# A fixed instruction order on every engine, a shorter distance between attention and input product, and an earlier set-up

## The chip, the cores and the metric

The kernel runs on one core of one Trainium2 chip. The metric is the device time of one execution in microseconds (us). A timed comparison has four runs of the kernel and four to seven runs of the kernel before, on the same chip. A ratio is the mean time of one kernel's fast runs over that of the other's of the same rounds, so it is not quite the ratio of the medians that are quoted beside it. The experiments ran on four chips, on which the kernel before took 435.4 to 436.0 us (medians); a difference between experiments of less than about 1 us is not read.

The names of the engines: PE is TensorE (PEld its weight loads), DVE is VectorE, ACT is ScalarE, POOL is GpSimd, SP is SyncE, which only issues transfers here.

## The reference, cut to what matters

```python
# r, k, v: (4, 8, 768, 48), w, u: (8, 48)
for t in range(S):
    cur = einsum('bhd,bhe->bhde', u * k_t, v_t)
    y_t = einsum('bhd,bhde->bhe', r_t, state + cur)
    state = w * state + einsum('bhd,bhe->bhde', k_t, v_t)
# y as (3072, 384); then
h = x @ w_in                       # 384 -> 1024
solu = h * softmax(h)
ln = (solu - mean) / sqrt(var + 1e-6) * g_ln
out = ln @ w_out                   # 1024 -> 384
```

The attention is done in 24 chunks of 128 tokens (four sequences of six). The two weight matrices arrive in 64-bit floating point and are converted on the chip, in 14 pieces.

## The kernel before

One round of the main loop handles attention chunk i, the input product and softmax of chunk i-LA, and the transposes and output product of chunk i-LA-LO. The parts that matter (cuts marked with "..."):

```python
LA, LO = 5, 3
psH = ...   # one buffer: the input product h_ps, 128x1024, fills it
psM = ...   # four buffers, shared by all other products and transposes but the scores

def convert(j):                                  # one weight piece
    nc.scalar.activation(out=mag, in_=hi..., func=ACT.Abs)            # ACT
    nc.vector.tensor_scalar(out=mag, ...)                             # DVE, clamp
    nc.vector.tensor_scalar(out=ma, ...)                              # DVE, shift
    nc.vector.scalar_tensor_tensor(out=ma, ...)                       # DVE, sign
    nc.scalar.activation(out=low, in_=lo, ...)                        # ACT
    if f is None:                                                     # w_in
        nc.gpsimd.tensor_tensor(out=dst..., in0=ma, in1=low, op=ALU.add)
    else:                                                             # w_out
        nc.gpsimd.tensor_tensor(out=ma, in0=ma, in1=low, op=ALU.add)  # POOL
        nc.scalar.activation(out=dst, in_=ma..., scale=g_sb[...])     # ACT, scaling

def weigh(i):
    nc.gpsimd.tensor_mul(kp..., kt..., kdec...)          # decayed k
    nc.gpsimd.tensor_mul(rku, kt[:, :, 0:D], u_bc)       # r*k*u, two products
    nc.gpsimd.tensor_mul(rku, rku, rt[:, :, 0:D])
    nc.vector.tensor_reduce(out=own[:, :, 0], in_=rku, ...)           # and their sum
    for h in range(H):                                   # eight diagonals: each token's own score, by head
        nc.scalar.activation(out=AT[:, h, :], in_=ident, scale=own[:, h])
...
with tc.manual_schedule(engines={mybir.EngineType.PE}):
    for i in range(-2, N + LA + LO):
        j, l = i - LA, i - LA - LO
        ...   # load(i+4), weigh(i+3), turn(i+2), conversions, then
        ...   # turn_ln(l), ffn_in(j), scores(i+1), ffn_out(l), finish(i)
```

`manual_schedule(engines={PE})` means: TensorE executes in the order of the program text, and a scheduler orders the instructions of the other engines.

## Time and profile before

| | before |
|---|---|
| time, median of 3 | 436.07 us |
| span of the profiled run | 433.0 us |
| mean granted TensorE clock | 0.991 |
| TensorE dense from | 102.07 us |
| one full round of TensorE | 16.08 us |

From the profile page of the kernel before, the busy times with their share of the span, and the chain of work that ended last, by engine:

```profile
PE 386.2 (89%) x2853; PEld 244.0 (56%) x2853; DVE 214.7 (50%) x386; ACT 181.6 (42%) x422; POOL 133.2 (31%) x165
...
PE 77%; POOL 8%; DVE 6%; issue 3%; ACT 2%; SPq 2%; DMA 1%; POOLq 0%; ACTq 0%; DVEq 0%
```

TensorE is the main bound: the chain runs through it for 77% of the span. What can be won without shortening TensorE's own work lies in the first quarter, where TensorE has holes; the other engines' shares are low on average but not there. The prediction below shows the slices and the table by stretch that say so.

### The profile page before, as it was taken

To read this page: it belongs to the slowest core of one execution; us is meant where nothing else is said; L and a number is where in the kernel's file an instruction comes from. 1 tells how busy PE (TensorE), PEld (TensorE's weight loads), DVE (VectorE), ACT (ScalarE), POOL (GpSimd) and SP (SyncE) were. 2 spreads that over 40 slices of the span, in tenths; PEclk is the share of its full clock that TensorE was granted. 3 is DMA by queue.
4 is the path that set the end of the run, shared out by engine and by line. 5 is a ranking of instruction groups with operands and counts; after the bars stand their busy time and mean duration, and the time that the engine had idled before them with its cause. 6 is when DMAs were issued, how large, how long until landed. Compare 5 with 4: busy or idle time off the path is not lost.

```text
span 433.0 us, 7179 instructions
## 1 busy us (share of the span) xinstructions
PE 386.2 (89%) x2853; PEld 244.0 (56%) x2853; DVE 214.7 (50%) x386; ACT 181.6 (42%) x422; POOL 133.2 (31%) x165
## 2 busy tenths in 40 slices
PE   0178692878999999999999999999999999999994
PEld 0167462445656656656756756756655565555662
DVE  5749885987453552552552542642544244444310
ACT  1667656765335435434434434533422233333310
POOL 5377686686134134134124113201000000000000
PEclk9999998899999999999999999999999999999999
DMA  9997989223033033033033011000000000000011
GB/s 147 232 242 148 157 193 173 27 56 56 20 56 74 18 56 73 20 56 73 20 55 73 24 34 38 20 2 18 20 0 20 20 20 18 18 18 19 0 39 42
DMA packets 81592, 25.92 MB, mean 60 GB/s; under 512 B 76557, under 2 KB 79758, under 8 KB 81550
## 3 DMA queue, kind: packets, MB, share of 16 engines
q1 hardware_dynamic: 80364, 25.17, 29.7%
q8 instruction: 24, 0.39, 0.4%
q10 hardware_dynamic: 1186, 0.20, 0.4%
q14 instruction: 18, 0.15, 0.1%
HBM read 20.65 MB, written 4.72 MB: 59 GB/s over the span
## 4 chain that ended last, share of the span: by engine, by line
PE 77%; POOL 8%; DVE 6%; issue 3%; ACT 2%; SPq 2%; DMA 1%; POOLq 0%; ACTq 0%; DVEq 0%
PE o_ps L737 29%; PE h_ps L698 27%; PE y_ps L668 7%; PE t_ps L726 5%; PE at L640 4%; PE kv_ps L684 3%; POOL kp L607 3%; POOL rku L612 2%; PE tr_ps L625 1%; POOL rku L611 1%; PE tk_ps L629 1%; DMA rpad<-in_r_dram 1%; DVE AT L643 1%; ACT AT L617 1%; SPq L462 1%
## 5 line engine op out<-in xcount | busy, mean ns | idle before, releaser
L698 PE MATMUL h_ps<-w_in_sb,xT 128*128 128x512 f32 x288 | 129.3, 599 | 11.7 <-DVE solu L708 11.7
L737 PE MATMUL o_ps<-w_out_sb,lnT 128*128 128x384 f32 x384 | 129.2, 490 | 0.0
L737 PEld LDWEIGHTS o_ps<-w_out_sb,lnT 128*128 128x128 f32 x384 | 71.5, 190 | 49.0 <-issue 2.4
L698 PEld LDWEIGHTS h_ps<-w_in_sb,xT 128*128 128x128 f32 x288 | 53.5, 193 | 70.4 <-issue 70.4
L704 ACT ACTIVATE e<-h_ps,st 128x1024 f32<-128x1024 f32 x24 | 26.7, 1114 | 116.9 <-DVE st L702 116.9
L713 POOL TENSOR_SCALAR st<-st 128x1 f32<-128x1 f32 x24 | 4.6, 192 | 193.3 <-ACT sq L712 193.1
L617 ACT ACTIVATE AT<-ident,own 128x128 f32<-128x128 f32 x192 | 59.1, 391 | 8.3 <-DVE own L614 8.3
L702 DVE TENSOR_REDUCE st<-h_ps 128x1 f32<-128x1024 f32 x24 | 29.4, 1223 | 60.3 <-PE h_ps L698 60.3
L712 ACT ACTIVATE sq<-solu,st 128x1024 f32<-128x1024 f32 x24 | 27.6, 1149 | 44.0 <-DVE st L710 44.0
L716 DVE TENSOR_SCALAR solu<-solu,st 128x1024 f32<-128x1024 f32 x24 | 21.5, 896 | 43.9 <-POOL st L715 43.9
L607 POOL TENSOR_TENSOR kp<-kpad,kdec 128x512 f32<-128x512 f32 x24 | 31.1, 1301 | 36.1 <-PE kv_ps L684 32.3
L640 PEld LDWEIGHTS at<-rT,kT 48*128 48x128 f32 x384 | 24.7, 189 | 22.9 <-issue 15.5
L640 PE MATMUL at<-rT,kT 48*128 48x128 f32 x384 | 30.0, 287 | 7.0 <-DVE AT L643 6.7
L614 DVE TENSOR_REDUCE own<-rku 128x8 f32<-128x384 f32 x24 | 13.1, 548 | 39.8 <-POOL rku L612 39.8
L643 DVE COPY_PREDICATED AT<-later,at 128x512 f32<-128x512 uint32 x48 | 32.3, 723 | 0.5 <-PE at L640 0.5
L708 DVE SCALAR_TENSOR_TENSOR solu<-h_ps,st,e 128x1024 f32<-128x1024 f32 x24 | 30.8, 1283 | 0.8
L612 POOL TENSOR_TENSOR rku<-rku,rpad 128x384 f32<-128x384 f32 x24 | 25.1, 1050 | 18.2 <-DMA rpad<-in_r_dram 17.5
L611 POOL TENSOR_TENSOR rku<-kpad,u_bc 128x384 f32<-128x384 f32 x24 | 25.9, 1079 | 7.0 <-DMA kpad<-in_k_dram 7.0
L726 PE MATMUL t_ps<-ident,solu 128*128 128x128 f32 x192 | 25.3, 274 | 1.7 <-DVE st L710 1.2
L668 PE MATMUL y_ps<-AT,vt 128*32 128x128 f32 x768 | 25.5, 273 | 0.0
L726 PEld LDWEIGHTS t_ps<-ident,solu 128*128 128x128 f32 x192 | 21.7, 141 | 5.2 <-issue 2.2
L684 PE MATMUL kv_ps<-vt,kp 128*128 128x96 f32 x160 | 22.6, 284 | 0.8 <-DVE state L690 0.8
(65 smaller groups left out, 358.7 us busy)
## 6 DMA issues: line engine op xcount, KB each, us to landing
kpad<-in_k_dram SPq DMA_DIRECT2D x24, 192.0 KB, 4.1
rpad<-in_r_dram SPq DMA_DIRECT2D x24, 192.0 KB, 5.0
vt<-in_v_dram SPq DMA_DIRECT2D x24, 192.0 KB, 3.0
out_dram<-o SPq DMA_DIRECT2D x24, 192.0 KB, 1.9
raw<-in_moe_w_in_dram SPq DMA_DIRECT2D x6, 512.0 KB, 5.2
raw<-in_moe_w_out_dram SPq DMA_DIRECT2D x8, 384.0 KB, 3.6
u_bc<-in_u_dram ACTq DMA_DIRECT2D x1, 192.0 KB, 3.8
g_sb<-in_moe_g_ln_dram ACTq DMA_DIRECT2D x1, 4.0 KB, 5.7
```

The lines of the kernel that those rows point to most:

```text
L607: nc.gpsimd.tensor_mul(kp.rearrange("p h d -> p (h d)"), kt.rearrange("p h d -> p (h d)"), kdec.rearrange("p a d -> p (a d)"))
L611: nc.gpsimd.tensor_mul(rku, kt[:, :, 0:D], u_bc)
L612: nc.gpsimd.tensor_mul(rku, rku, rt[:, :, 0:D])
L617: nc.scalar.activation(out=AT[:, h, :], in_=ident, func=ACT.Copy, scale=own[:, h])
L640: nc.tensor.matmul(pss[q][:, a, :], X["kT"][rows, a, :], X["rT"][rows, a, :], start=True, stop=True)
L643: nc.vector.copy_predicated(A4[:, :, q, :], later.to_broadcast([128, HP, T]), pss[q])
L668: nc.tensor.matmul(y_ps[32 * g : 32 * g + 32, j, :], lhsT, rhs, start=(g not in opened), stop=stop, skip_group_check=True)
L684: nc.tensor.matmul(kv_ps[:, a], pair(X["kp"], a), vt[:, 2 * a : 2 * a + 2, 0:D], start=True, stop=True)
L698: nc.tensor.matmul(h_ps[:, ts(n, NX)], X["xT"][:, j, :], w_in_sb[:, j, ts(n, NX)], start=(j == 0), stop=(j == KD - 1))
L708: nc.vector.scalar_tensor_tensor(out=solu, in0=h_ps, scalar=rs, in1=e, op0=ALU.mult, op1=ALU.mult, accum_out=tot)
L726: nc.tensor.transpose(t_ps[:, f, :], X["solu"][:, ts(4 * g + f, 128)], ident)
L737: nc.tensor.matmul(o_ps, X["lnT"][:, f, :], w_out_sb[:, f, :], start=(f == 0), stop=(f == KF - 1))
```

## The change

Its intent: take the order of all engines out of the scheduler's hands, so that the tables are made while GpSimd rests and the w_in pieces are converted first; and bring the input product from five chunks behind attention to two, so that full rounds begin three rounds sooner. (The decay row was the first transfer in the text before, too; the scheduler issued it third, at 2.19 us.) Its core:

```diff
-    LA, LO = 5, 3
+    LA, LO = 2, 3
+    ctx.enter_context(tc.manual_schedule())
...
+    nc.sync.dma_start(out=wq[:, :, 0:D], in_=w...)      # decay row: now the first transfer
...
-    load(0, "kr"); ...; load_weights(0); load(1, "v"); load(2); load_weights(1); ...
+    load(0, "kr"); load_weights(0); load(1, "kr"); load(0, "v"); load_weights(1); ...
...
+    double(0)                     # decay table for k first, then its transposes,
+    ...                           # then reciprocals and double(1), the table for r
...
-    with tc.manual_schedule(engines={mybir.EngineType.PE}):
-        for i in range(-2, N + LA + LO):
+    conversions = {-2: 1, -1: 1, 0: 2, 1: 2, 2: 3, 3: 3, 4: 2}
+    for i in range(-2, N + LA + LO):
+        ...                                  # load, turn_r
+        if i <= 0: weigh_own(i + 2, nc.vector)
+        turn_k(i + 2)
+        decay_k(i + 3)
+        for _ in range(conversions.get(i, 0)): convert(todo.pop(0)); ...
+        diagonal(i + 2)
+        turn_ln(l)
+        ffn_in(j)                            # input product, maximum, exponential
+        scores(i + 1)
+        unit(j)                              # reciprocal, product, square, root
+        weigh_own(i + 3, nc.gpsimd)          # two products, and DVE's sum
+        ffn_out(l)
+        normalise(j)
+        finish(i)                            # attention product, copy xT, state
```

In the changed kernel this text is the queue of every engine.

More of the change, by code (lines that the diff above doesn't have):

```diff
@@ L451, in direct_path @@
     vts = [const.tile([128, H, D + 32], F32, name=f"vt{i}") for i in range(NV)]
-    for i in range(NLD):
-        nc.vector.memset(kpads[i][:, :, D:P], 0.0)
-        nc.vector.memset(rpads[i][:, :, D:P], 0.0)
-    for vt in vts:
-        nc.gpsimd.memset(vt[:, :, D:], 0.0)
     def load(i, which="krv"):
@@ L472, in direct_path @@
     nc.vector.memset(wq, 1.0)
+    nc.sync.dma_start(out=wq[:, :, 0:D], in_=w.rearrange("(a q) d -> a q d", q=2))
+    nc.scalar.dma_start(out=u_bc.rearrange("p h d -> p (h d)"),
+                        in_=u.rearrange("h d -> (h d)").partition_broadcast(128))
+    for i in range(NLD):
+        nc.vector.memset(kpads[i][:, :, D:P], 0.0)
+        nc.vector.memset(rpads[i][:, :, D:P], 0.0)
     def words(x):
@@ L517, in convert @@
                                  scale=g_sb[:, f : f + 1])
-    nc.sync.dma_start(out=wq[:, :, 0:D], in_=w.rearrange("(a q) d -> a q d", q=2))
     load(0, "kr")
-    nc.scalar.dma_start(out=u_bc.rearrange("p h d -> p (h d)"),
-                        in_=u.rearrange("h d -> (h d)").partition_broadcast(128))
+    load_weights(0)
     load(1, "kr")
     load(0, "v")
-    load_weights(0)
+    load_weights(1)
     load(1, "v")
-    load(2)
-    load_weights(1)
+    load_weights(2)
+    load(2, "kr")
+    load_weights(3)
+    load(2, "v")
+    load_weights(4)
     load(3)
-    load_weights(2)
-    nc.scalar.dma_start(out=g_sb, in_=moe_g_ln.rearrange("(c p) -> p c", p=128))
-    nc.scalar.dma_start(out=wrow, in_=w.rearrange("h d -> (h d)").partition_broadcast(1))
     ident = const.tile([128, 128], F32, name="ident")
     make_identity(nc, ident)
+    for vt in vts:
+        nc.gpsimd.memset(vt[:, :, D:], 0.0)
     neg_half = const.tile([128, 1], F32, name="neg_half")
-    nc.vector.memset(neg_half, -0.5)
+    nc.gpsimd.memset(neg_half, -0.5)
     tab = const.tile([128, 2, HP, T], F32, name="tab")
@@ L544, in direct_path, with double @@
     pw = const.tile([128, 2, 8, HP], F32, name="pw")
+    nc.vector.memset(back[:, :, T - 1 : T], 1.0)
+    def double(x):
+        for j in range(7):
+            n = 1 << j
+            nc.vector.tensor_mul(tab[:, x, :, T - 2 * n : T - n], tab[:, x, :, T - n : T],
+                                 pw[:, x, j].unsqueeze(2).to_broadcast([128, HP, n]))
     wd_ps = psM.tile([128, HP], F32, tag="m", name="wd_ps")
     nc.tensor.transpose(wd_ps, wq.rearrange("a q d -> a (q d)"), ident[0:HP, 0:HP])
-    nc.vector.memset(back[:, :, T - 1 : T], 1.0)
     nc.vector.tensor_scalar(out=pw[:, 0, 0], in0=wd_ps, scalar1=LOW, scalar2=HIGH,
@@ L551, in direct_path @@
         nc.vector.tensor_mul(pw[:, 0, j + 1], pw[:, 0, j], pw[:, 0, j])
-    nc.vector.reciprocal(out=pw[:, 1], in_=pw[:, 0])
-    nc.vector.tensor_copy(out=fore[:, :, T - 1 : T], in_=pw[:, 1, 0].unsqueeze(2))
-    for j in range(7):
-        n = 1 << j
-        step = pw[:, :, j].unsqueeze(3).to_broadcast([128, 2, HP, n])
-        nc.vector.tensor_mul(tab[:, :, :, T - 2 * n : T - n], tab[:, :, :, T - n : T], step)
+    double(0)
     kdec = const.tile([128, HP, 128], F32, name="kdec")
@@ L564, in direct_path @@
     nc.scalar.copy(out=kdec, in_=kd_ps)
+    nc.vector.reciprocal(out=pw[:, 1], in_=pw[:, 0])
+    nc.vector.tensor_copy(out=fore[:, :, T - 1 : T], in_=pw[:, 1, 0].unsqueeze(2))
+    double(1)
     later = const.tile([128, 1, T], U32, name="later")
@@ L571, in direct_path, with make_wt @@
                             pattern=[[1, T]], channel_multiplier=-1)
-    nc.vector.tensor_copy(out=later[:, 0, :], in_=mf)
+    nc.gpsimd.tensor_copy(out=later[:, 0, :], in_=mf)
+    states = [const.tile([128, HP, 2, D], F32, name=f"state{b}") for b in range(B)]
     wt = const.tile([128, HP, 2, D], F32, name="wt")
-    nc.gpsimd.memset(wt, 0.0)
-    for q in range(2):
-        rows = slice(q * P, q * P + D)
-        nc.vector.tensor_copy(out=wt[rows, :, q, :],
-                              in_=pw[rows, 0, 7].unsqueeze(2).to_broadcast([D, HP, D]))
-    states = [const.tile([128, HP, 2, D], F32, name=f"state{b}") for b in range(B)]
+    def make_wt():
+        nc.gpsimd.memset(wt, 0.0)
+        for q in range(2):
+            rows = slice(q * P, q * P + D)
+            nc.gpsimd.tensor_copy(out=wt[rows, :, q, :],
+                                  in_=pw[rows, 0, 7].unsqueeze(2).to_broadcast([D, HP, D]))
     bad = flag.tile([1, 1], mybir.dt.int32, name="bad")
     def check_range():
+        nc.sync.dma_start(out=wrow, in_=w.rearrange("h d -> (h d)").partition_broadcast(1))
         ok = small.tile([1, dm], F32, tag="ok", name="ok", bufs=1)
@@ L600, in pair, with decay_k, weigh_own, diagonal @@
         return t[:, 2 * a : 2 * a + 2, :].rearrange("p q d -> p (q d)")
-    def weigh(i):
-        kt, rt = kpads[i % NLD], rpads[i % NLD]
+    def decay_k(i):
         X = live[i] = {}
-        X["kp"] = kp = apool.tile([128, H, P], F32, name="kp", bufs=4)
-        nc.gpsimd.tensor_mul(kp.rearrange("p h d -> p (h d)"),
-                             kt.rearrange("p h d -> p (h d)"),
+        X["kp"] = apool.tile([128, H, P], F32, name="kp", bufs=4)
+        nc.gpsimd.tensor_mul(X["kp"].rearrange("p h d -> p (h d)"),
+                             kpads[i % NLD].rearrange("p h d -> p (h d)"),
                              kdec.rearrange("p a d -> p (a d)"))
+    def weigh_own(i, engine):
         rku = apool.tile([128, H, D], F32, name="rku")
-        nc.gpsimd.tensor_mul(rku, kt[:, :, 0:D], u_bc)
-        nc.gpsimd.tensor_mul(rku, rku, rt[:, :, 0:D])
-        own = small.tile([128, H, 1], F32, name="own")
+        engine.tensor_mul(rku, kpads[i % NLD][:, :, 0:D], u_bc)
+        engine.tensor_mul(rku, rku, rpads[i % NLD][:, :, 0:D])
+        own = live[i]["own"] = small.tile([128, H, 1], F32, name="own")
         nc.vector.tensor_reduce(out=own[:, :, 0], in_=rku, axis=AX.X, op=ALU.add)
-        AT = X["AT"] = apool.tile([128, H, T], F32, name="AT", bufs=4)
+    def diagonal(i):
+        X = live[i]
+        AT = X["AT"] = apool.tile([128, H, T], F32, name="AT", bufs=3)
         for h in range(H):
-            nc.scalar.activation(out=AT[:, h, :], in_=ident, func=ACT.Copy, scale=own[:, h])
-    def turn(i):
-        X, rt = live[i], rpads[i % NLD]
-        X["kT"] = apool.tile([128, HP, T], F32, name="kT")
-        X["rT"] = apool.tile([128, HP, T], F32, name="rT", bufs=3)
+            nc.scalar.activation(out=AT[:, h, :], in_=ident, func=ACT.Copy, scale=X["own"][:, h])
+    def turn_r(i):
+        rT = live[i]["rT"] = apool.tile([128, HP, T], F32, name="rT", bufs=3)
         ps = psM.tile([128, HP, T], F32, tag="m", name="tr_ps")
         for a in range(HP):
-            nc.tensor.transpose(ps[:, a, :], pair(rt, a), ident)
-        nc.vector.tensor_mul(X["rT"], ps, fore)
+            nc.tensor.transpose(ps[:, a, :], pair(rpads[i % NLD], a), ident)
+        nc.vector.tensor_mul(rT, ps, fore)
+    def turn_k(i):
+        X = live[i]
+        X["kT"] = apool.tile([128, HP, T], F32, name="kT")
         ps = psM.tile([128, HP, T], F32, tag="m", name="tk_ps")
@@ L700, in ffn_in @@
         st = small.tile([128, 8], F32, name="st")
-        nmax, se, rs, tot, nmu, ss, var, rstd = (st[:, n : n + 1] for n in range(8))
+        nmax, se, rs, tot, nmu, ss, var, rstd = X["st"] = [st[:, n : n + 1] for n in range(8)]
         nc.vector.tensor_reduce(out=nmax, in_=h_ps, axis=AX.X, op=ALU.max, negate=True)
@@ L704, in ffn_in, with unit @@
         nc.scalar.activation(out=e, in_=h_ps, func=ACT.Exp, bias=nmax, accum_out=se)
+        X["h"], X["e"] = h_ps, e
+    def unit(i):
+        X = live[i]
+        nmax, se, rs, tot, nmu, ss, var, rstd = X["st"]
+        h_ps, e = X["h"], X["e"]
         nc.vector.tensor_scalar_add(rs, se, 1e-9)
@@ L715, in ffn_in, with normalise @@
         nc.gpsimd.tensor_tensor(out=rstd, in0=var, in1=neg_half, op=ALU.pow)
-        nc.vector.tensor_scalar(out=solu, in0=solu, scalar1=nmu, scalar2=rstd,
+    def normalise(i):
+        X = live[i]
+        nmax, se, rs, tot, nmu, ss, var, rstd = X["st"]
+        nc.vector.tensor_scalar(out=X["solu"], in0=X["solu"], scalar1=nmu, scalar2=rstd,
                                 op0=ALU.add, op1=ALU.mult)
@@ L745, in direct_path @@
     todo = list(range(len(pieces)))
-    count = {5: 3, 6: 3, 7: 2}
-    ahead = 3
-    weigh(0)
-    weigh(1)
-    with tc.manual_schedule(engines={mybir.EngineType.PE}):
-        for i in range(-2, N + LA + LO):
-            j, l = i - LA, i - LA - LO
-            if 0 <= i and i + 4 < N:
-                load(i + 4)
-            if 0 <= i + 3 and i + 3 < N and i + 3 >= 2:
-                weigh(i + 3)
-            if 0 <= i + 2 < N:
-                turn(i + 2)
-            for _ in range(count.get(i, 1)):
-                if i >= -1 and todo:
-                    convert(todo.pop(0))
-                if ahead < len(pieces):
-                    load_weights(ahead)
-                    ahead += 1
-            if i == 10:
-                check_range()
-            if 0 <= l < N and i < N + LA:
-                turn_ln(l)
-            if 0 <= j < N:
-                ffn_in(j)
-            if 0 <= i + 1 < N:
-                scores(i + 1)
-            if N + LA - 1 <= i < N + LA + LO - 1:
-                turn_ln(l + 1)
-            if 0 <= l < N:
-                ffn_out(l)
-            if 0 <= i < N:
-                finish(i)
+    ahead = 5
@@ new lines, in direct_path @@
+    conversions = {-2: 1, -1: 1, 0: 2, 1: 2, 2: 3, 3: 3, 4: 2}
+    decay_k(0)
+    for i in range(-2, N + LA + LO):
+        j, l = i - LA, i - LA - LO
+        drain = i >= N + LA - 1
+        if 0 <= i and i + 4 < N:
+            load(i + 4)
+        if i + 2 < N:
+            turn_r(i + 2)
+            if i <= 0:
+                weigh_own(i + 2, nc.vector)
+            turn_k(i + 2)
+        if i + 3 < N:
+            decay_k(i + 3)
+        if i == -2:
+            make_wt()
+        for _ in range(conversions.get(i, 0)):
+            convert(todo.pop(0))
+            if ahead < len(pieces):
+                load_weights(ahead)
+                ahead += 1
+        if i + 2 < N:
+            diagonal(i + 2)
+        if i == 0:
+            nc.sync.dma_start(out=g_sb, in_=moe_g_ln.rearrange("(c p) -> p c", p=128))
+        if i == 10:
+            check_range()
+        if 0 <= l and not (drain and i > N + LA - 1):
+            turn_ln(l)
+        if 0 <= j < N:
+            ffn_in(j)
+        if 0 <= i + 1 < N:
+            scores(i + 1)
+        if 0 <= j < N:
+            unit(j)
+        if 0 <= i and i + 3 < N:
+            weigh_own(i + 3, nc.gpsimd)
+        if drain and l + 1 < N:
+            turn_ln(l + 1)
+        if 0 <= l:
+            ffn_out(l)
+        if 0 <= j < N:
+            normalise(j)
+        if 0 <= i < N:
+            finish(i)
```

## The prediction

> **What bounds the kernel now.** I read the page from the top: busy shares, slices, then the chain of waits, then who waited for whom, then each engine's instructions in order of time for the first 105 us and for one round of the middle.
>
> ```profile
> PE   0178692878999999999999999999999999999994
> DVE  5749885987453552552552542642544244444310
> PEclk9999998899999999999999999999999999999999
> DMA  9997989223033033033033011000000000000011
> ```
>
> One slice is 10.8 us. From the tenth on, TensorE is full; the ten before it are the ramp, where TensorE has holes and DVE, ACT, GpSimd and the DMA are busy in turn. The busy table by stretch puts numbers to it (columns: PE, PE weight loads, DVE, ACT, POOL busy, clock, DMA share, GB/s).
>
> ```profile
> 0.00:19.07 19.07, 0.24 (x2) 0.18 (x2) 14.12 (x42) 7.02 (x19) 9.34 (x21) 1.00 1.12 180
> 19.07:56.50 37.43, 28.45 (x374) 24.06 (x375) 26.12 (x41) 25.21 (x65) 26.50 (x22) 1.00 0.99 193
> 56.50:102.07 45.57, 33.35 (x316) 21.37 (x315) 35.79 (x62) 28.78 (x71) 34.09 (x34) 0.93 0.52 93
> 102.07:310.70 208.63, 207.47 (x1597) 130.93 (x1597) 97.75 (x170) 87.82 (x209) 57.30 (x72) 1.00 0.21 41
> 310.70:427.40 116.70, 116.67 (x572) 67.46 (x568) 40.91 (x72) 32.28 (x58) 5.93 (x16) 1.00 0.06 19
> ```
>
> So after 102.07 us nothing but TensorE's own work counts, and before it everything else does. One full round of TensorE, from the chain of waits: transposes of the output side 0.87, input product 5.15, scores 1.09, output product 5.36, attention product 1.67, state product 1.06, transposes of r and k 0.44 each, together 16.08 us. In the ramp TensorE waited for:
>
> ```profile
> PE h_ps L698 <- DVE solu L708: 11.7, 2, 8.8
> PE kd_ps L563 <- DVE tab L557: 11.5, 1, 11.5
> PE wd_ps L546 <- POOL rku L611: 7.3, 1, 7.3
> PE at L640 <- DVE AT L643: 6.7, 4, 2.6
> ```
>
> The first 19 us are table making; the last hole is the input product waiting for the softmax of the chunk before it, which holds its only PSUM tile.
>
> **What the skill says.** "PSUM — Partial Sum Buffer", section "Engine vs sequencer instructions": the queues of ScalarE, VectorE and GpSimd are strictly first in, first out. The trace of before can't contradict it, since a scheduler chose the order there; under a fixed order it means that one instruction which waits stops all written after it. "SBUF — State Buffer", section "SBUF: two separate sides": VectorE and GpSimd share a port pair as an exclusive lock. The trace agrees: the clamp of a weight piece takes 0.43 us alone and 1.50 us when it starts at 33.34 beside a GpSimd product that ends at 34.55. "TensorE: Matmul & The Clock Gate", section "What's actually happening": after an idle window TensorE runs at half clock for about 3.4 us. Here the input product after the 8.8 us hole took 6.96 us, the next ones 5.3.
>
> **The change part by part.** Round i holds attention chunk i; the input product is now of chunk i-2 (before i-5), the output product still three behind it. So full rounds begin at round 5, not 8. TensorE's work from the start of round 5 on: 15 full rounds (5 to 19) 241.1, then rounds that lose the state product, transposes, scores and attention, 15.0+15.0+14.1+13.0+11.2+12.1+6.0+6.0+5.2 = 97.6, together 338.7. (Check by the same sum for before: 12 full rounds and 131.2 make 324.1; 102.07 plus 1.3 of waits plus 324.1 is 427.5, measured 427.4.) After it come 5.6 us of eviction and store, and the time is 3.1 above the profiled span (436.07 against 433.0). The time after is T5 + 338.7 + waits + 8.7, and the change gains only if round 5 starts before 88.7 us less any new waits.
>
> *Start.* The decay row is now the first transfer on its queue (before: 2.19 us, behind 384 KB, used at 7.26), so I take it at 4.2. GpSimd only clears buffers then, so the seven squarings cost 0.19 each, not 0.56, and seven half-size doublings about 2.0: the first table at 8.2 in place of 19.07, its transposed copy at 10, the first scores at 13 (before 24.96). About 11 us gained.
>
> *Rounds 0 and 1.* DVE runs in program order: turned r 0.68, for the first three chunks also two products (0.55 each) and the sum (0.55), conversions of a w_in piece 1.53 each, masks 1.34, the sum of r·k·u, which from chunk 3 on waits for GpSimd (two weight additions 1.27 each, then two products 1.05 each), the state 0.54. With the port lock I get the end of DVE's round 0 at 33, of round 1 at 43. TensorE's first input product ends near 40.5 (before 63.4).
>
> *Rounds 2 to 4: the w_out conversions.*
>
> ```profile
> L501 ACT ACTIVATE mag<-raw 128x384 f32<-128x384 f32 x8 | 4.4, 546 | 0.0
> L502 DVE TENSOR_SCALAR mag<-mag 128x384 f32<-128x384 f32 x8 | 5.7, 714 | 2.7 <-ACT mag L501 2.6
> L508 DVE SCALAR_TENSOR_TENSOR ma<-raw,ma 128x384 uint32<-128x384 uint32 x8 | 7.0, 870 | 0.1
> L515 POOL TENSOR_TENSOR ma<-ma,low 128x384 uint32<-128x384 uint32 x8 | 8.1, 1017 | 6.5 <-DVE ma L508 3.3 <-ACT low L511 2.0 <-DVE st L706 1.0
> L516 ACT ACTIVATE w_out_sb<-ma,g_sb 128x384 f32<-128x384 f32 x8 | 4.9, 612 | 5.3 <-POOL ma L515 5.3
> ```
>
> Each piece goes ACT, DVE, GpSimd, ACT. In the fixed order ACT does magnitude, low word, scaling of one piece before the magnitude of the next, and the scaling waits for GpSimd. So pieces no longer overlap: 0.55 + 0.36 + 0.35 + 0.56 (uncontended) + 1.0 + 0.61 and some 0.25 of hops is 3.7 us each. Behind them in the same queues stand, in order, DVE's maximum 1.22; ACT's eight diagonals 2.45 after the last scaling; the exponential 1.3; DVE's reciprocal and product 1.75; ACT's square 1.35; GpSimd's variance and root 0.85, two products 2.1; DVE's sum, normalisation and state 2.0. A round with three pieces: 0.7 + 1.3 to the first addition + 1.05 + 0.65 + 2 x 3.7 + 2.45 + 1.3 + 1.75 + 1.35 + 0.85 + 2.1 + 2.0 = 22.9; with two, 19.2. DVE's rounds 2, 3, 4 end at about 66, 89, 108. TensorE needs 10 us in each and waits for the product that frees the input product's PSUM tile: the input products start near 59, 82 and 101 to 104, the last being the one of round 5. Taking 1.75 of transposes off, round 5 starts at 102.5, and 1.5 us for the half clock makes 104.
>
> *Full rounds.*
>
> ```profile
> 228.38 0.55 POOL L715 TENSOR_TENSOR st<-st,neg_half 128x1 f32<-128x1 f32 x1
> 228.97 0.81 DVE L716 TENSOR_SCALAR solu<-solu,st 128x1024 f32<-128x1024 f32 x1 [2.28 <-POOL st L715]
> 231.44 0.56 DVE L687 TENSOR_TENSOR state<-kv_ps,state 128x384 f32<-128x384 f32 x1 [1.66 <-PE kv_ps L684]
> ```
>
> Here DVE waits for TensorE before the state; the scheduler had put the sum of r·k·u elsewhere (220.64). Now GpSimd makes its two products after the root, and DVE has sum, normalisation, state in that order. From the end of the input product (222.23): root at 6.7, products 8.85, sum 9.45, normalisation 10.25, state 10.8. In the compiled program the second group of output-side transposes waits for that state addition (its PSUM tile is the state product's), and TensorE gets there at 10.3. That closes a loop of 10.85 + 0.44 + 5.35 = 16.64 against 16.08: 0.56 a round in 15 rounds, 8.5 us.
>
> Sum: 104 + 338.7 + 8.5 + 8.7 = 460 us, 24 above before.
>
> **Rivals.** (a) The shorter ramp wins: three attention-only rounds vanish and the tables come 11 us sooner; if the conversions overlapped, round 5 could start near 75 and the time be some 422. For it: the first hole is real, and the first input product comes 20 us sooner. Against: the compiled order has no overlap left. (b) The DMA sets the ramp: 6.3 MB of double-width weights plus eight chunks, 4.7 MB, take some 46 us at the 240 GB/s seen; needed in order, they land before the conversions I place at 43 to 94, so it costs nothing; with slower delivery the rounds 0 and 1 would slip 5 us. (c) Full rounds stay at 16.08 because waits are shorter than I count: then about 451. (d) Nothing changes: gain at the start and loss in the conversions cancel, 436; it needs rounds 2 to 4 at 15 us each, about what before took with its scheduler (55 to 98 us for rounds 5 to 7).
>
> **Range and chances.** The start may be off by 3 us, rounds 0 and 1 by 5, rounds 2 to 4 by 8, the full rounds by 5; together some 11. I say 460, with 449 to 471 for eight in ten. Faster would need 27 us of error in the same direction: 0.08; within 2%: 0.07; slower: 0.85.
>
> **What would show it.** Right: first table transpose near 8 us; ACT waiting for GpSimd before each w_out scaling and eight conversions about 3.7 us apart; input products near 59, 82 and 103; clock dips there; a period of 16.6 us in the middle with TensorE's transposes waiting for DVE's state. Wrong: full TensorE slices before 90 us, a period of 16.1, or conversions that overlap.

## The result, and the profile after

The changed kernel takes 454.32 us (median of 4 runs, 453.92 to 454.42) against 435.9 us: ratio 1.0426, 95% interval 1.0406 to 1.0446. Predicted were 460.0, with 449 to 471.

The page of the changed kernel: busy times, TensorE's slices (one is 11.3 us), the granted clock by slice, and the chain.

```profile
PE 399.3 (88%) x2853; PEld 248.9 (55%) x2853; DVE 207.5 (46%) x395; ACT 183.2 (40%) x422; POOL 125.4 (28%) x163
...
PE   2598081829999999999999999999999999999995
...
PEclk9879677677999999999999999999999999999999
...
PE 46%; DVE 25%; POOL 12%; ACT 9%; issue 6%; DMA 1%; POOLq 0%; ACTq 0%; DVEq 0%
```

Read three things. TensorE starts early now (2, 5, 9 instead of 0, 1, 7). Then come three holes, in slices 5, 7 and 9, before the full row begins. And the same 2853 matmuls keep TensorE busy for 13 us longer: a larger busy time is no more work here. The input product has 5.2 us of it (134.5 for 129.3), where the clock row is down at 6 and 7 around the holes; the output-side transposes have 4.0 (29.3 for 25.3), mostly a wait inside their records that is shown below. The chain has moved from TensorE to the other three engines: 46% in place of 77%.

The busy table of three stretches of the changed kernel (columns as in the prediction: PE, PE weight loads, DVE, ACT, POOL, clock, DMA share, GB/s):

```profile
0.00:42.20 42.20, 28.48 (x233) 21.41 (x233) 33.60 (x76) 22.68 (x55) 23.94 (x35) 0.88 1.06 220
42.20:101.98 59.78, 26.48 (x200) 15.77 (x192) 28.55 (x57) 27.25 (x64) 16.20 (x21) 0.73 0.30 53
101.98:447.00 345.02, 343.58 (x2427) 211.58 (x2428) 145.34 (x263) 132.77 (x303) 85.30 (x109) 0.99 0.19 38
```

In the middle stretch no engine is busy for half of the time, and the DMA is not either. Such a stretch is bound by nobody's speed: everybody waits for everybody in turn. Who for whom, from the table of waits of the changed kernel (total us, times, longest):

```profile
DVE own L627 <- POOL rku L625: 86.6, 21, 4.3
...
ACT w_out_sb L518 <- POOL ma L517: 31.6, 8, 7.9
...
PE h_ps L716 <- DVE solu L732: 25.2, 2, 14.1
...
PE t_ps L754 <- ACT xT L698: 8.1, 1, 8.1
...
PEld t_ps L754 <- DVE state L705: 5.0, 15, 0.3
```

The third and fourth lines are TensorE's holes. The second is one of the things that stretch them: eight times, once for each w_out piece, ACT stands in front of a scaling until GpSimd has added. The first pieces of it, in ACT's order of time (start, duration, idle time before and what ended it):

```profile
45.20 0.61 ACT L518 ACTIVATE w_out_sb<-ma,g_sb 128x384 f32<-128x384 f32 x1 [7.94 <-POOL ma L517]
45.72 0.53 ACT L503 ACTIVATE mag<-raw 128x384 f32<-128x384 f32 x1
46.15 0.54 ACT L513 ACTIVATE low<-raw 128x384 uint32<-128x384 uint32 x1
48.79 0.61 ACT L518 ACTIVATE w_out_sb<-ma,g_sb 128x384 f32<-128x384 f32 x1 [2.11 <-POOL ma L517]
```

The magnitude of the next piece (45.72) needs nothing of the scaling (45.20), but stands behind it in ACT's queue; DVE gets its work from that magnitude, GpSimd from DVE, and ACT waits again. Scalings follow at 48.79 and 52.48: 3.6 us a piece.

The fifth line of the waits is the small one that comes back in the full rounds. One of them, on DVE and then on TensorE:

```profile
217.75 0.55 DVE L627 TENSOR_REDUCE own<-rku 128x8 f32<-128x384 f32 x1 [4.33 <-POOL rku L625]
218.22 0.80 DVE L744 TENSOR_SCALAR solu<-solu,st 128x1024 f32<-128x1024 f32 x1
218.94 0.55 DVE L705 TENSOR_TENSOR state<-kv_ps,state 128x384 f32<-128x384 f32 x1
```
```profile
218.84 1.36 PE L754 MATMUL t_ps<-ident,solu 128*128 128x128 f32 x8
```

DVE idles 4.33 us in front of a sum, for GpSimd's products. Behind it stand the normalisation, ready since GpSimd's root ended at 215.67, and the state addition, ready when the state product ends near 218.1. The state addition frees the PSUM tile that the second half of the output-side transposes needs, so those take 1.36 us where they took 1.04, and this round 16.40 us (the first ones 16.34) where TensorE's own work is 16.08.

### The profile page after: what moved, and what is told of

It is laid out like the page before. It is cut to its first block, busy times and chain, and to the rows that moved or that the text cites. A ratio compares the mean times of both kernels' runs of the same rounds, so it can differ in the third digit from the quotient of the medians.

```text
span 452.7 us, 7184 instructions
## 1 busy us (share of the span) xinstructions
PE 399.3 (88%) x2853; PEld 248.9 (55%) x2853; DVE 207.5 (46%) x395; ACT 183.2 (40%) x422; POOL 125.4 (28%) x163
## 4 chain that ended last, share of the span: by engine, by line
PE 46%; DVE 25%; POOL 12%; ACT 9%; issue 6%; DMA 1%; POOLq 0%; ACTq 0%; DVEq 0%
PE h_ps L716 24%; PE o_ps L765 13%; DVE solu L732 5%; PE t_ps L754 4%; ACT e L722 4%; POOL rku L625 4%; POOL rku L624 4%; DVE st L720 4%; DVE solu L744 3%; DVE own L627 2%; PE y_ps L686 2%; POOL st L739 2%; ACT sq L736 2%; POOL ma L517 2%; DVE ma L510 2%
## 5 line engine op out<-in xcount | busy, mean ns | idle before, releaser
L716 PE MATMUL h_ps<-w_in_sb,xT 128*128 128x512 f32 x288 | 134.5, 618 | 25.6 <-DVE solu L732 25.2
L716 PEld LDWEIGHTS h_ps<-w_in_sb,xT 128*128 128x128 f32 x288 | 55.3, 199 | 87.9 <-issue 86.7
L754 PE MATMUL t_ps<-ident,solu 128*128 128x128 f32 x192 | 29.3, 284 | 9.5 <-ACT xT L698 8.1
L658 PEld LDWEIGHTS at<-rT,kT 48*128 48x128 f32 x384 | 25.7, 198 | 19.8 <-issue 19.0
L744 DVE TENSOR_SCALAR solu<-solu,st 128x1024 f32<-128x1024 f32 x24 | 20.3, 845 | 10.8 <-POOL st L739 10.8
L648 ACT COPY kT<-tk_ps 128x512 f32<-128x512 f32 x24 | 14.0, 583 | 26.6 <-PE tk_ps L647 26.6
L706 POOL TENSOR_TENSOR state<-state,wt 128x384 f32<-128x384 f32 x16 | 16.0, 1002 | 29.7 <-DVE state L705 29.7
```

The costliest lines, as they stand in the source:

```text
L658: nc.tensor.matmul(pss[q][:, a, :], X["kT"][rows, a, :], X["rT"][rows, a, :], start=True, stop=True)
L716: nc.tensor.matmul(h_ps[:, ts(n, NX)], X["xT"][:, j, :], w_in_sb[:, j, ts(n, NX)], start=(j == 0), stop=(j == KD - 1))
L744: nc.vector.tensor_scalar(out=X["solu"], in0=X["solu"], scalar1=nmu, scalar2=rstd, op0=ALU.add, op1=ALU.mult)
L754: nc.tensor.transpose(t_ps[:, f, :], X["solu"][:, ts(4 * g + f, 128)], ident)
```

## The experiments

All twelve gave correct results. The theory, A: the order costs the time. Three places in it stop a queue on a late operand, and the distance of two chunks itself is no harm. The main rival, B: the short distance costs the time, since it puts the softmax into the rounds in which the weights are converted, whatever the order.

**e1_pipe: the scaling one piece later on ACT.** ACT now does magnitude and low word of the next piece before the scaling of the last.

```diff
-            convert(todo.pop(0))
+            now = convert(todo.pop(0))      # returns its scaling, not yet issued
+            if scaling: scaling()
+            scaling = now
...
+        if scaling: scaling()
```

> Edit: in the fixed order, the scaling of a w_out piece on ACT comes one piece later, after the magnitude and low word of the next piece. Theory A (the conversions are serialised by ACT's order: each scaling waits for GpSimd, and the next magnitude stands behind it): the pieces of a round overlap, 3.6 us between them becomes about 2.2 (DVE 1.27 plus GpSimd 1.0 under the port lock), five such gaps in rounds 2 to 4, so about 7 us off: 447 us. Theory B (the lag of two chunks is itself too short, the holes are the softmax chain from one input product to the next): under 2 us off, 453.

Measured: 447.20 us, ratio 1.0273 (1.0249 to 1.0296), 7.1 below the changed kernel. ACT's scalings in this run:

```profile
45.49 0.62 ACT L518 ACTIVATE w_out_sb<-ma,g_sb 128x384 f32<-128x384 f32 x1 [5.52 <-POOL ma L517]
...
47.45 0.61 ACT L518 ACTIVATE w_out_sb<-ma,g_sb 128x384 f32<-128x384 f32 x1 [0.47 <-POOL ma L517]
...
49.88 0.61 ACT L518 ACTIVATE w_out_sb<-ma,g_sb 128x384 f32<-128x384 f32 x1 [1.82 <-POOL ma L517]
```

A piece takes 2.2 us now ((49.88 - 45.49) / 2) and not 3.6, and the later input products start 2.6, 5.5 and 7.1 us sooner (55.79, 75.64, 96.61 for 58.38, 81.13, 103.74). The last figure is the gain in time: five gaps between pieces, each 1.4 us shorter.

**e2_state: DVE's sum of r·k·u after the state addition.**

```diff
-            weigh_own(i + 3, nc.gpsimd)
+            add_own = weigh_own(i + 3, nc.gpsimd)     # the two products; the sum is returned
...
             finish(i)
+            add_own()
```

> Edit: DVE's sum of r*k*u stands after the state addition instead of before the normalisation. Theory A: the second output-side transpose no longer waits for a late state addition, the period of full rounds goes from 16.4 to 16.08 us, 15 rounds, 4.8 us off: 449.6 us; the ramp stays. Theory C (the longer period comes from something else, such as the half clock or the weight loads): 454, period 16.4.

Measured: 445.71 us, ratio 1.0238 (1.0211 to 1.0264), 8.6 below the changed kernel. The period in the full rounds is exactly 16.08 us (output-side transposes at 116.24, 132.31, 148.39), so the loop in the full rounds is the one that the prediction named. In a full round of DVE:

```profile
212.02 0.56 DVE L705 TENSOR_TENSOR state<-kv_ps,state 128x384 f32<-128x384 f32 x1 [0.97 <-PE kv_ps L702]
212.49 0.54 DVE L627 TENSOR_REDUCE own<-rku 128x8 f32<-128x384 f32 x1
```

The sum waits no more. The gain was 4 us larger than expected, since the same wait also sits in the ramp: in round 2 DVE had idled 4.26 us before the sum; now 0.42, and the normalisation starts at 60.00 and not at 63.16. The sum of it: 4.7 in 15 full rounds (0.26 to 0.33 each), 3.3 by an earlier round 5 (98.68 for 101.98), and 1.1 because the input product after it ran less at half clock (5.91 for 6.98), together 9.1. The spans of the two profiled runs differ by 9.0 (452.7 and 443.7), the medians by 8.6.

**e3_diag: ACT's eight diagonals after the exponential and the square, from round 2 on.**

```diff
-        if i + 2 < N:
+        if i + 2 < N and j < 0:
             diagonal(i + 2)
...
             unit(j)
+        if i + 2 < N and j >= 0:
+            diagonal(i + 2)
```

> Edit: from round 2 on, ACT writes the eight diagonals after the exponential and the square instead of before. Theory A: in rounds 2 to 4 the exponential stands 2.45 us less far behind the last scaling, so each of the three rounds is 2.4 us shorter, 7 us off in all: 447 us; full rounds keep 16.4. Theory B: the same direction, since this is in the softmax chain, so this run tells the size only. Theory D (DVE, not ACT, sets these rounds): no change, 454.

Measured: 451.65 us, ratio 1.0367 (1.0343 to 1.0392): 2.7 gained of the 7 expected. A miss in size, and the trace shows why. The input products of rounds 3 and 4 start 2.1 and 4.4 us sooner, but then:

```profile
97.58 1.11 PE L754 MATMUL t_ps<-ident,solu 128*128 128x128 f32 x4 [8.80 <-ACT xT L698]
```

The copy of the attention output (xT) stands behind the 2.4 us of diagonals now, and TensorE needs that copy to come into round 5. The wait was moved to another instruction of the same queue, not taken away.

**e4_sched: the scheduler orders all engines but TensorE.** Everything else of the change stays.

```diff
-    ctx.enter_context(tc.manual_schedule())
+    ctx.enter_context(tc.manual_schedule(engines={mybir.EngineType.PE}))
```

> Edit: the changed kernel, but with only TensorE in fixed order; the other engines are ordered by the scheduler as in the kernel before. Theory A: the scheduler overlaps the conversions and the chain again, the lag of two is a gain, and the time falls under 440 us, perhaps to 425 to 435. Theory B (the lag of two is at fault): it stays over 448.

Measured: 429.06 us, ratio 0.9853 (0.9831 to 0.9875). This decides between A and B for the two-chunk distance: with the same distance, loads and work, a freer order is 25.3 us faster than the fixed one, and faster than the kernel before. Its two largest waits of TensorE:

```profile
PE h_ps L716 <- DVE solu L732: 9.7, 2, 7.3
PE kd_ps L567 <- DVE tab L552: 9.4, 1, 9.4
```

The two holes before input products are 9.7 us together where they were 25.2. On the other hand the tables are late: the scheduler puts products and conversions among the squarings, and the first table transpose comes at 15.42 us, not at 7.23. That looks like 8 us left to win.

**e5_three: the three reorderings together, all in a fixed order.** The edit is the sum of the three diffs above.

> The three reorderings together (scaling one piece later, sum after the state, diagonals after exponential and square), all in a fixed order. If their gains are independent: 454.3 minus 7.1, 8.6 and 2.7 makes 436, within 2 us of the kernel before. If they mostly take away the same wait (the input product waiting for the softmax of the chunk before): 440 to 444. The period in the full rounds is 16.08 in both cases.

Measured: 435.02 us, ratio 0.9994 (0.9975 to 1.0012). The separate gains add up (18.4 expected, 19.3 found): they are, for the most part, three different waits.

**e6_la5: the changed kernel in its fixed order, with five chunks of distance.**

```diff
-    LA, LO = 2, 3
+    LA, LO = 5, 3
```

> The changed kernel in its fixed order, but with the input product five chunks behind attention again. Theory A (the order costs the time, not the distance): the conversions still do not overlap, 3.7 us apart, and three more rounds come before the full ones; 448 to 460. Theory B (the short distance costs the time, because it puts the softmax into the rounds of the conversions): 440 or less.

Measured: 445.59 us, ratio 1.0245 (1.022 to 1.027), between the two ranges: A had asked for 448 or more, B for 440 or less. So neither holds alone. The w_out scalings are still 3.6 us apart (45.33, 48.92, 52.63), which is A's part; but the conversion rounds follow each other in 14.5 and 14.1 us (first scalings at 45.33, 59.79, 73.91), in the changed kernel in 22.7 and 22.7 (45.20, 67.93, 90.66), since no softmax stands behind the conversions (the first input product starts at 75.94, after the last scaling but one), which is B's. In this order the short distance costs 8.7 us.

**e7_wqlate: the decay row behind the first chunk's k and r on its queue.**

```diff
-    nc.sync.dma_start(out=wq[:, :, 0:D], in_=w...)
     ...
     load(0, "kr")
+    nc.sync.dma_start(out=wq[:, :, 0:D], in_=w...)
```

> The changed kernel with the decay row behind the first chunk's k and r on its queue again: the tables come 2 to 3.7 us later. If the early start reaches the end of the kernel one to one: 456.3 to 458. If it is swallowed by a later wait in the ramp (conversions, data): 454.3, the same.

Measured: 457.59 us, ratio 1.0509 (1.0492 to 1.0527): 3.3 slower than the changed kernel. The first table transpose comes 2.8 us later (10.03), and each of the four input products of the ramp 3.1 us later (37.35, 61.44, 84.19, 106.82). In the fixed order the ramp is one chain, and a delay at its head reaches the end undiminished.

**e9_hybrid0: fixed order for the tables and the rounds -2 and -1, scheduler from round 0.** It was to win the 8 us that the run with the scheduler seemed to leave.

```diff
     for i in range(-2, N + LA + LO):
+        if i == 0:
+            ...     # leave the fixed order, fix TensorE alone
```

> The fixed order for the tables and the rounds -2 and -1 only; from round 0 on only TensorE's order is fixed and the other engines are ordered by the scheduler, as in the run before this. First transpose for the decay table near 7.3 us instead of 15.4. If the start counts to the end: 429.1 minus about 8 makes 421. If the conversions bound the ramp from there on, whatever the start: 426 to 429. The period stays 16.08.

Measured: 428.58 us, ratio 0.9846 (0.983 to 0.9863), not told apart from the 429.06 with the scheduler throughout, and in the range that was set for a ramp bound by the conversions. The tables are 6.7 us sooner (8.73), but the first input product only 2.7 (36.81 for 39.49) and round 5 only 2.0 (80.91 for 82.92). The scheduler's late tables had not been idle time: products and conversions were done in between, which here come after. Set beside the run before: how much a start is worth depends on whether what comes after it is one chain (there tables 2.8 us later put everything 3.1 us later) or a pool of work that can be shuffled (here tables 6.7 us sooner put round 5 2.0 us sooner).

**e10_la5sched: five chunks, scheduler.** The fourth corner of distance and order; both edits are shown above.

> The fourth corner: input product five chunks behind attention and only TensorE in a fixed order. The kernel is then close to the kernel before, with the changed set-up. If the shorter distance is a gain once the other engines are free: 431 to 436 here, against 429.1 with two chunks. If the distance does nothing in a free order: 428 to 430. If the fixed order alone makes the distance harmful (two chunks 8.7 worse than five there), the sign turns here.

Measured: 433.28 us, ratio 0.9939 (0.9909 to 0.997). The four corners, with the start of the output-side transposes in the first full round (from there on TensorE has, by the prediction's sums, 338.7 us of work with two chunks and 324.1 with five):

| | fixed order, all engines | only TensorE fixed |
|---|---|---|
| distance 5 | 445.59 us (110.22) | 433.28 us (103.39) |
| distance 2 | 454.32 us (101.98) | 429.06 us (82.92) |

The sign of the distance turns with the order. Step by step: the changed set-up and text with the old distance, 433.28 for 435.64 us; the shorter distance in a free order, another 4.2 less; the order of all engines fixed, 25.3 more. With a free order, full rounds begin 20.5 us sooner for 14.6 us more work after them, so the shorter distance wins; in the fixed order they begin only 8.2 us sooner, so it loses.

**e11_defer: a better fixed order.** To the scaling one piece later and the sum after the state come two moves: the normalisation of a chunk stands one round later (the transposes need it only two rounds after that), and the diagonals at the end of a round, behind xT.

```diff
+        if 0 <= j - 1 < N:
+            normalise(j - 1)
...
-        if 0 <= j < N:
-            normalise(j)
             finish(i)
+        if i + 2 < N and j >= 0:
+            diagonal(i + 2)
```

> All engines in a fixed order, with the scaling one piece later and the sum after the state, and two more moves: the normalisation of a chunk one round later (its output transposes come only two rounds after), and the eight diagonals at the end of a round, behind the copy of the attention output. In the run with three reorderings DVE waited 2.2 us a round for GpSimd before the normalisation, and that copy stood behind 2.4 us of diagonals. If a bad order is the cause and not the fixing of it: full rounds begin near 80 instead of 86.75 and the time is 427 to 431, level with the scheduler. If a fixed order can't follow the varying arrival times: 434 to 436, no better than the three reorderings.

Measured: 428.92 us, ratio 0.984 (0.9806 to 0.9873), level with the scheduler; round 5 starts at 82.71. Fixing the order is not the fault, this order was. What DVE still waits for, in one round of this run:

```profile
72.31 0.55 DVE L627 TENSOR_REDUCE own<-rku 128x8 f32<-128x384 f32 x1 [3.07 <-POOL rku L625]
```

**e13_early: GpSimd's two products before the variance and the root**, where it idles for ACT's square.

```diff
+        add_own = weigh_own(i + 3, nc.gpsimd)    # after the conversions
...
         unit(j)
...
-        add_own = weigh_own(i + 3, nc.gpsimd)
```

> As the run with the deferred normalisation, but GpSimd's two products for r*k*u stand before its variance and root, where it idles some 5 us for the square, not after them. In that run DVE waited 3.1 to 3.8 us a round for these products before its sum. If that is the last wait that a fixed order adds: full rounds begin near 76 instead of 82.7 and the time is 421 to 425, which beats all kernels so far. If the ramp is bound by the loop of the input product's PSUM tile instead, or the products collide with DVE's conversions: 427 to 429.

Measured: 428.37 us, ratio 0.9826 (0.9801 to 0.9851), no gain that can be told from the run before. The number falls into the rival's range. Of its two reasons the first holds in part: the input products still wait for their PSUM tile (7.52 and 3.08 us), but that loop has a wait in it that can be moved, as the next run shows. The wait for GpSimd is gone, as meant, and DVE's next wait in the same round is nearly as long:

```profile
72.81 0.36 DVE L504 TENSOR_SCALAR mag<-mag 128x384 f32<-128x384 f32 x1 [2.69 <-ACT mag L503]
```

DVE waits for ACT's magnitude of the next piece, which stands behind xT, eight diagonals (69.42 to 71.86) and the copy of the transposed k. The bound passed from GpSimd to ACT.

**e14_split: the diagonals in ACT's gaps**, one round later: three before the first scaling, five before the last.

```diff
+        split = [range(0, 3), range(3, 8)] if i >= 3 and i + 1 < N else []
...          # in the conversions, ahead of the first scaling:
+                if len(split) == 2: diagonal(i + 1, split.pop(0))
...          # ahead of the last:
+        while split: diagonal(i + 1, split.pop(0))
...
-        if i + 2 < N and j >= 0: diagonal(i + 2)
```

> As the run before, but the eight diagonals of a chunk stand on ACT one round later, in the gaps where ACT waits for GpSimd between the conversions (three before the first scaling, five before the last), not between the copy of the attention output and the next magnitude. In the run before, DVE waited 2.7 to 3.4 us a round for that magnitude, which stood behind 2.4 us of diagonals: ACT had become the bound. If that is so: about 2.4 us less in each of rounds 3 and 4 and in the start of round 5, full rounds from 76 to 78, and 422 to 425. If another wait takes its place at once, as in the run before: 427 to 429.

Measured: 424.52 us, ratio 0.9752 (0.9723 to 0.9782): the fastest of all, 29.8 us below the changed kernel with the same instructions, the same distance and every engine in a fixed order. TensorE comes into its first full round:

```profile
78.95 1.17 PE L756 MATMUL t_ps<-ident,solu 128*128 128x128 f32 x8 [0.95 <-DVE state L707]
79.95 5.32 PE L718 MATMUL h_ps<-w_in_sb,xT 128*128 128x512 f32 x12
```

The start is at 78.95, a little later than the 76 to 78 expected. The input product takes 5.32 us, so the clock is full; in the changed kernel it came after a hole and took 6.98. From 40 us to there, DVE is busy for 33.45 of 38.95 us, in the changed kernel for 18.43 of the same stretch: little waiting is left on DVE. Making its work shorter was not tried.

## Why the prediction was right

Right in direction, in the mechanism and in the range; the point was 5.7 us too high. By its own steps:

| step | predicted | measured |
|---|---|---|
| decay row there, first table transpose | 4.2, 8.2 us | 3.60, 7.23 |
| first scores | 13 | 13.11 |
| end of DVE's rounds 0, 1 | 33, 43 | 33.1, 42.2 |
| w_out pieces apart | 3.7 | 3.6 |
| input products of rounds 3, 4, 5 | 59, 82, 101 to 104 | 58.38, 81.13, 103.74 |
| end of DVE's rounds 2, 3, 4 | 66, 89, 108 | 64.9, 87.6, 106.3 |
| full rounds, T5 with half clock | 104 | 101.98 + 2.6 |
| TensorE's work from round 5 on | 338.7 | 338.5, see below |
| loss in 15 full rounds | 0.56 each, 8.5 | 0.26 to 0.33 each, 4.7 |
| eviction, store, time over span | 5.6 + 3.1 | 4.9 + 1.6 |

The 2.6 is what round 5 takes above 16.08 (18.63 us): 0.9 in the transposes and 1.7 in the input product, both at a lower clock. The 338.5 is from the run with the sum after the state, which has no loss in its full rounds: 15 rounds of 16.08, then 97.4 to the end of the last matmul. The measured terms close: 101.98 + 2.6 + 338.5 + 4.7 + 4.9 = 452.7, the span of the profiled run. The run with the scheduler checks the 338.5: 82.92, 0.8 of waits in round 5, 338.5, and 5.0 after the last matmul make 427.2, against a span of 427.3.

*What was mis-sized.* Of the 5.7 us, 3.8 are the full rounds. The prediction laid the sum, the normalisation and the state addition end to end and put the state's end at 10.85 us after the input product. In the trace each starts before the one ahead has ended in the records (217.75 + 0.55 is 218.30, the next starts at 218.22), so the state addition ends 10.5 us after the input product (219.49 for 208.96). The trace of before shows such an overlap too (state addition 215.37 + 0.56, the next at 215.84). The loop closes in 16.40 us in this round, where 16.64 was predicted: in a term of 0.56 us, a quarter of a microsecond is nearly half. Another 1.5 is the difference between the time and the span. The prediction set the median of other executions (436.07) against the span of the profiled one (433.0); that execution itself took 434.72, 1.7 above its span, and in the changed kernel the difference is 1.6. The rest nearly cancels: the tail after the last matmul was 0.7 shorter, and round 5 lost 0.5 more than the start and its half clock were given, since the prediction charged the half clock to the input product alone and not to the transposes before it.

*What the Trainium skill said, and the runs.* "PSUM — Partial Sum Buffer", section "Engine vs sequencer instructions", has the three other queues strictly first in, first out. The prediction rested on it, and the runs agree: moving one instruction in one queue gained 7.1 us on ACT and 8.6 us on DVE. "SBUF — State Buffer", section "SBUF: two separate sides" (under "Who interferes with whom"), says which DVE instructions GpSimd can block: those in a two-port mode, and those with two SBUF inputs while GpSimd reads SBUF. In the run with the scheduler the second kind shows: the sign step of a w_out piece took 0.56 us alone and 1.55 us (median of two) when it began beside a running GpSimd instruction, while the multiplication of r, whose one input is in PSUM, took 0.68 us in both cases.

*The rivals of the prediction.* (a), that a shorter ramp wins and the time is 422 if conversions overlap and round 5 starts near 75, was wrong for this kernel and right for its better orders: 424.52 with round 5 at 78.95. The prediction gave the condition for it and saw in the compiled order that it was not met. (b), that the DMA sets the ramp: after 42 us its share is 0.30, and no hole of TensorE there ends on a transfer. (c), full rounds at 16.08 and a time of 451, has the nearer number (3.3 us off, against 5.7), but by its mechanism it is wrong: the loop exists, with about half of its predicted size. (d), gain and loss cancel, would have needed rounds of 15 us; rounds 2, 3 and 4 took 22.7, 22.7 and 18.7 (from DVE's ends in the table).

What stays open: the experiments don't tell how much of the 8.7 us that two chunks cost against five in the fixed order lies in the conversions and how much in the other waits of rounds 2 to 4.

## What to carry to other kernels

In a fixed order, an instruction that waits holds everything behind it in its queue, ready or not: before each one that takes its operand from another engine, put what is ready already, and move what isn't needed soon (a sum, a normalisation, a scaling) behind it or a round later. Taking one such wait away often uncovers the next of the same size on another engine, so look for the new wait before you judge the idea. A structural change (here the distance) can't be judged apart from the order: it lost 8.7 us in one order and won 4.2 us in another.

## What the Trainium skill lacked or had wrong

- "TensorE: Matmul & The Clock Gate", section "What's actually happening", says that what is issued in the first 3.4 us or so runs at half clock, and that for a model the ramp penalty is below 1% of a typical span. Input products after a hole took 6.98, 7.53 and 8.10 us in the changed kernel, and 8.34 in one experiment, against 5.32; the granted clock in them was 0.76, 0.71, 0.66 and 0.64. If the excess is half clock, the half clock lasted 3.3 to 6.0 us in them (an estimate: twice the excess). Before the 6.98 stand transposes at a clock of 0.50 for 1.76 us, so in this hole's case it lasted 5.1. In the changed kernel that is an excess of 2.2, 2.8 and 2.6 us, 7.6 of 454 us or 1.7%, for three holes.
- "PSUM — Partial Sum Buffer", section "Engine vs sequencer instructions", says that the queues are first in, first out; no page says what an order is worth. Here the same instructions took 454.32 us in one fixed order and 424.52 us in another.
- "Perfetto Trace Analysis", section "Identifying the Most-Contended Engine", has the engine with the highest occupancy optimized first. In the stretch from 42.2 to 101.98 us of the changed kernel no engine reaches one half (DVE 28.55 us of 59.78, ACT 27.25, TensorE 26.48, GpSimd 16.20), and a better order shortened the stretch that corresponds to it to 37.5 us (41.4, where DVE's round 1 ends, to 78.95). Taken alone, occupancy doesn't point to a cause that is in the order of waits.
